# Attention's last weight steps taken apart, constants moved behind attention, and `gated @ w_out` begun in three PSUM banks without its last row block

## The chip, the cores and the metric

One core of one Trainium2 chip runs the whole program. The metric is device time in microseconds. The kernel before takes 1671.38 us (median of 3 runs, 1671.3 to 1676.62).

## The reference

Three stages follow one another on 8 batches of 576 tokens, all in float32:

```python
# attention (8 heads of 64, 128 features and their negatives)
proj = x @ w_phi;  proj = proj - max(abs(proj))
phi = concat([exp(proj), exp(-proj)])
out = (phi(q) @ (phi(k).T @ v)) / (phi(q) @ sum(phi(k)) + 1e-6)
# gated MLP
h = relu(x @ w_in);  u, v = h[..., :512], h[..., 512:]
v_n = (v - mean(v)) / sqrt(var(v) + 1e-6)
gated = u * (w_spatial @ v_n + b_spatial)
x = gated @ w_out
# mixer
u = x + (low-rank token mixing of x by U, V)
out = u + relu(u @ w_ch1) @ w_ch2
```

## The kernel before, in words

Every product of float32 operands is made of three matmuls on rounded halves: an operand is split into a high part (a copy in fp32r) and a low part (the operand less its high part), and `products` (L661) issues high x high, high x low and low x high for each row block. The functions below are named by their lines in the kernel before.

**Attention** (`attention`, L557) is a loop of 36 steps over 32 pairs of heads, in which four pairs are at different points of their way. A step projects k of the next pair (`pk`), forms the numerator and denominator of older pairs in four groups (`pn`, one bank; the copy out of it into `nd`, by DVE for group 1 and by ACT for the others, frees the bank for the next group), transposes q (`pt`) and projects q of the next pair (`pq`). DVE takes the maximum and the difference of each projection (`mk` and `sk`, `mq` and `sq`), splits the key-value product (`kv`) and copies `nd`. These are pinned: they keep the order in which the program writes them.

The weights of the next stage are brought in during these steps by a list of jobs (`weight_jobs`, L169). A job is a chain of functions; each call does one piece and returns the next. `step` calls a piece at three places of a loop step: after `less()` and `taken()` near the start, after the key features, and at the end of a step. A function marked `late` is only called at the end of a step. What is called there is put behind the newest pinned instruction of each engine (`behind`), and a new job starts at the end of a step when the last has finished. The job of the last rows of `w_spatial` and of the bias has two late pieces: `bias` (L216: ACT copies the high part, DVE subtracts, DVE clears a buffer, SP loads the bias into it) and `bias_split` (L230: ACT copies, DVE subtracts).

**Constants.** `alloc_moe` (L641) clears a buffer `w_pad`, sets two rows of it to 1 and casts it into the last rows of `vn[1]` (L653 to L656). The buffer is the weights' staging buffer. Nothing ties these instructions to a place: the scheduler that orders each engine's instructions decides.

**Gated MLP.** For each batch `gate` (L761) forms u (`pu`, four blocks f) and `w_spatial @ v_n` (`pz`, four blocks f), multiplies them and splits the product into `gs` by its four row blocks. A list of jobs runs beside it: batches 1 to 6 bring in five or six pieces of `w_ch1` and `w_ch2` each (load 512 KB, repack by ACT and DVE, store), one call of `work` behind each of the eight blocks f. Then `gated_out` (L822) makes the five token tiles of `gated @ w_out`: four of 128 tokens (`px_0` to `px_3`, 12 matmuls each, row blocks 0 to 3 in turn) and the tail (`px_4`, 8 matmuls). Each is copied by ACT to `x` and split by DVE into `xh` and `xl`, which the low-rank product `pr` reads. `pu`, `pz`, `pv`, `px` and `pt` share four PSUM banks in rotation. Between these, `values` (L711) makes v and its normal form for the next batch (`pv`, `vn`); on its path DVE and POOL (the reciprocal root `rstd`, and the low part of `vn`) alternate. In the last batch the first parts of the channel stage (`us`, `cw`) are formed on ACT and DVE at the same time.

**Channel mixing** (`channel`) follows and takes the rest of the span, from about 903 us.

## Time and profile before

| what | value |
|---|---|
| median of 3 runs | 1671.38 us |
| profiled execution | 1671.03 us, span 1669.2 us |
| PE busy | 1614.8 us, 97% of the span |
| DVE, ACT, POOL busy | 64%, 45%, 25% |
| PE's granted clock, mean | 0.988 |

The span is one profiled execution; 1.83 us of its time lie outside the span. A busy share near 100% says that the engine almost always had an instruction in hand, not that it ran at its full clock: the granted clock of a stretch (PEclk in the windows) tells that, 1.00 being 2.4 GHz and 0.50 being 1.2 GHz. What can be saved without fewer matmuls is PE's idle time and the stretches at the lower clock.

### The profile page before, as it was taken

Reading aid. Unit: us, or ns where it says so; the run is one execution under the profiler, and the core shown is the slowest. Engines: PE = TensorE matmul, PEld = TensorE weight load, DVE = VectorE, ACT = ScalarE, POOL = GpSimd, SP = SyncE. Lnnn points to the kernel's source line nnn. Section 1 sums busy time; section 2 is a strip of 40 time slices with the busy share of each in tenths; the row PEclk is TensorE's granted clock in tenths of the full one; section 3 lists DMA queues with packets and bytes.
Section 4 is the critical chain, followed back from the end, with each engine's and each line's share of the span. In section 5 each row is a group of like instructions: output and inputs, shape, how many; then the busy total and the mean of one; then the engine's idle time right before and its main releaser. Section 6 shows DMA issues by size and latency. Waiting matters only on the chain.

```text
span 1669.2 us, 28381 instructions
## 1 busy us (share of the span) xinstructions
PE 1614.8 (97%) x10968; PEld 1447.7 (87%) x10968; DVE 1072.7 (64%) x1997; ACT 744.4 (45%) x1343; POOL 421.6 (25%) x354
## 2 busy tenths in 40 slices
PE   7999998998999999999998999999999999999999
PEld 7998987887888898888897899999889999988897
DVE  6888756874567567566638885757475756565654
ACT  5888765773444443443424442323232323232322
POOL 3677774765342252342320000000000000000000
PEclk9999998999999999999999999999999999999999
DMA  4667664652132432431214441313132323232221
GB/s 136 197 198 211 202 189 125 198 148 87 59 114 86 142 109 72 123 114 62 89 46 135 130 151 52 124 54 118 60 112 65 103 72 98 71 101 76 68 85 39
DMA packets 118475, 184.53 MB, mean 111 GB/s; under 512 B 23810, under 2 KB 52642, under 8 KB 118340
## 3 DMA queue, kind: packets, MB, share of 16 engines
q1 hardware_dynamic: 118196, 182.66, 35.6%
q8 instruction: 86, 1.41, 0.4%
q14 instruction: 49, 0.40, 0.1%
q10 hardware_dynamic: 144, 0.07, 0.0%
HBM read 136.24 MB, written 36.85 MB: 104 GB/s over the span
## 4 chain that ended last, share of the span: by engine, by line
PE 72%; DMA 11%; DVE 6%; ACT 5%; issue 3%; POOL 2%; SPq 1%; DVEq 0%; POOLq 0%; ACTq 0%
PE pc L667 23%; PE ph L667 20%; DMA raw_c<-in_w_ch 5%; PE pv L667 4%; PE pn L508 4%; PE pu L667 4%; PE px L667 4%; PE pkv L480 3%; PE pk L407 2%; PE pt L439 1%; PE pt L872 1%; PE pq L407 1%; PE pz L667 1%; PE py L876 1%; DMA k<-in_kT 1%
## 5 line engine op out<-in xcount | busy, mean ns | idle before, releaser
L667 PE MATMUL pc<-h,w 128*128 128x512 f32 x1728 | 423.8, 394 | 1.5 <-ACT w L137 1.0
L667 PEld LDWEIGHTS ph<-us,cw 128*128 128x128 f32 x3024 | 384.7, 190 | 20.4 <-DVE u L993 3.1
L667 PE MATMUL ph<-us,cw 128*128 128x256 f32 x3024 | 390.0, 283 | 5.5 <-DVE u L993 4.2
L667 PEld LDWEIGHTS pc<-h,w 128*128 128x128 f32 x1728 | 314.4, 188 | 64.7 <-ACT w L137 1.2
L998 ACT ACTIVATE h<-c 128x256 fp32r<-128x256 f32 x288 | 114.6, 418 | 314.2 <-DVE c L993 307.6
L508 PE MATMUL pn<-qp,kv 128*65 128x288 f32 x768 | 211.6, 335 | 14.8 <-DVE nd L517 11.2
L461 POOL TENSOR_TENSOR qp<-e,qp 128x576 fp32r<-128x576 f32 x128 | 184.4, 1461 | 135.8 <-ACT e L458 104.3
L993 DVE TENSOR_TENSOR c<-ph,u 128x256 f32<-128x256 f32 x216 | 90.9, 422 | 111.9 <-PE ph L667 109.3
L480 PE MATMUL pkv<-v,kp 128*128 128x65 f32 x1024 | 156.9, 257 | 0.0
L480 PEld LDWEIGHTS pkv<-v,kp 128*128 128x128 f32 x1024 | 156.5, 197 | 0.0
L993 DVE TENSOR_TENSOR u<-ph,u 128x256 f32<-128x256 f32 x144 | 60.4, 422 | 146.6 <-PE ph L667 144.8
L137 ACT CAST w<-w2r 128x1024 fp32r<-128x1024 f32 x72 | 75.7, 1051 | 119.1 <-PE pc L667 106.8
L999 DVE SCALAR_TENSOR_TENSOR h<-c,h 128x256 fp32r<-128x256 f32 x288 | 115.2, 421 | 17.2 <-ACT h L998 13.4
L508 PEld LDWEIGHTS pn<-qp,kv 128*65 128x65 f32 x768 | 101.5, 143 | 21.1 <-DVE nd L517 13.0
L667 PE MATMUL pz<-wt,vn 128*128 128x288 f32 x768 | 112.3, 295 | 1.5 <-DVE u L813 1.5
L667 PE MATMUL pu<-xs,wi 128*128 128x288 f32 x768 | 105.0, 298 | 2.1 <-DVE v L730 2.1
L667 PEld LDWEIGHTS pu<-xs,wi 128*128 128x128 f32 x768 | 104.3, 190 | 3.1 <-DVE v L730 2.4
L667 PEld LDWEIGHTS pz<-wt,vn 128*128 128x128 f32 x768 | 105.3, 188 | 2.0 <-DVE u L813 2.0
L667 PE MATMUL px<-wo,g 128*128 128x512 f32 x384 | 92.4, 398 | 9.4 <-ACT g L137 9.4
L667 PEld LDWEIGHTS px<-wo,g 128*128 128x128 f32 x384 | 71.8, 191 | 27.6 <-ACT g L137 12.0
L667 PE MATMUL pv<-wi,xs 128*128 128x512 f32 x384 | 92.2, 394 | 0.0
L140 DVE TENSOR_TENSOR w<-w2r,w 128x1024 fp32r<-128x1024 f32 x72 | 88.1, 1224 | 3.1 <-ACT w L137 3.1
(150 smaller groups left out, 2255.3 us busy)
## 6 DMA issues: line engine op xcount, KB each, us to landing
w2r<-w2d SPq DMA_DIRECT2D x144, 256.0 KB, 3.0
raw_c<-in_w_ch SPq DMA_DIRECT2D x32, 512.0 KB, 4.3
v<-in_v SPq DMA_DIRECT2D x32, 325.0 KB, 4.0
k<-in_kT SPq DMA_DIRECT2D x32, 320.0 KB, 3.6
q<-in_qT SPq DMA_DIRECT2D x32, 320.0 KB, 4.1
x<-nd SPq DMA_DIRECT2D x64, 144.0 KB, 3.4
rec<-rd SPq DMA_DIRECT2D x64, 144.0 KB, 3.1
xd<-x SPq DMA_DIRECT2D x32, 288.0 KB, 2.5
```

The costliest lines, as they stand in the source:

```text
L137: nc.scalar.copy(hi, src)
L140: return (nc.gpsimd if elo == "pool" else nc.vector).tensor_tensor(out=lo, in0=src, in1=hi, op=ALU.subtract)
L407: self.pin(nc.tensor.matmul(pa[:, j * NF + t, :], x[d, t * P : (t + 1) * P], ws[d, :], start=True, stop=True,))
L439: self.pin(nc.tensor.transpose(pt[:, at, :], s[:, u, :], self.ident))
L461: self.pin(nc.gpsimd.tensor_tensor(out=lo[:, c], in0=e[:, c], in1=hi[:, c], op=ALU.subtract))
L480: self.pin(nc.tensor.matmul(pkv[:, i, j, :], kp[:, j * NF + t, :], vb[:, u * D1 : (u + 1) * D1], start=False, stop=(j == 1 and t == NF - 1),))
L508: self.pin(nc.tensor.matmul(pn, kv[k][:, i, g // 2, :], qp[q][:, i, g * HS : (g + 1) * HS], start=(m == 0), stop=(m == len(terms) - 1),))
L667: self.nc.tensor.matmul(out, x, y, start=(start and i == 0), stop=(stop and i == len(terms) - 1))
L872: nc.tensor.transpose(pt[:, s0 - c0 : s0 - c0 + n], ts[t][0][:n, fs], self.ident[:n, :n])
L993: nc.vector.tensor_tensor(out=out, in0=p, in1=q, op=ALU.add)
L998: nc.scalar.activation(hi, src, AF.Relu)
L999: nc.vector.scalar_tensor_tensor(out=lo, in0=src, scalar=0.0, in1=hi, op0=ALU.max, op1=ALU.subtract)
```

## The change

Three edits. First, in attention, the two late pieces of the bias job are cut in two, so that only ACT's copies are late; DVE's subtractions (and the clearing of the buffer with SP's load behind it) become pieces of their own that may run at the next place. Secondly, the constants of `vn` are put behind attention's last pinned instructions. Thirdly, the first three token tiles of `gated @ w_out` are opened in three banks with the row blocks 0 to 2 each, and then take row block 3 in turn; with this, the calls of `work` behind the last two blocks f move behind the low-rank product and between the two halves of `mixed`.

```diff
--- before.py
+++ after.py
@@ -119,7 +119,7 @@
         self.tail = self.S - self.NF * P
         self.NST = self.NF + 1
         self.ST = [(i * P, min(P, self.S - i * P)) for i in range(self.NST)]
-        self.pending, self.last = None, [None] * 4
+        self.pending, self.last, self.rest = None, [None] * 4, []
         dp = ctx.enter_context(tc.tile_pool(name="dp", bufs=1, space=DRAM))
         B, S = self.B, self.S
         self.xd = [dp.tile([P, self.KD, S], F32, name=f"xd{b}") for b in range(B)]
@@ -213,8 +213,15 @@
             for i in range(2):
                 nc.sync.dma_start(w[i * tail : (i + 1) * tail, :], self.w_spT[NF * P :, :])
 
+            def late(f):
+                f.late = True
+                return f
+
             def bias():
                 nc.scalar.copy(wt0, w)
+                return less
+
+            def less():
                 nc.vector.tensor_tensor(
                     out=wt1[:tail, :], in0=w[:tail, :], in1=wt0[:tail, :], op=ALU.subtract
                 )
@@ -223,14 +230,15 @@
                 for i in range(2):
                     r = tail + i * 32
                     nc.sync.dma_start(b[r : r + 1, :], self.b_sp)
-                f = lambda: bias_split(b)
-                f.late = True
-                return f
-
-            def bias_split(b):
+                return late(lambda: bias_parts(b))
+
+            def bias_parts(b):
                 for i in range(2):
                     r = slice(tail + i * 32, tail + (i + 1) * 32)
                     nc.scalar.copy(wt1[r, :], b[r, :])
+                return lambda: bias_less(b, r)
+
+            def bias_less(b, r):
                 nc.vector.tensor_tensor(
                     out=wt1[r, :], in0=b[r, :], in1=wt1[r, :], op=ALU.subtract
                 )
@@ -650,10 +658,11 @@
 
         self.vn = [mq.tile([P, self.NST, self.DH], F32R, name=f"vn{i}") for i in range(2)]
         pad = self.stage("pad", self.DH)
-        nc.vector.memset(pad[tail:, :], 0.0)
-        for r in (tail, tail + 32):
-            nc.vector.memset(pad[r : r + 1, :], 1.0)
-        nc.vector.tensor_copy(self.vn[1][tail:, NF, :], pad[tail:, :])
+        with self.behind():
+            nc.vector.memset(pad[tail:, :], 0.0)
+            for r in (tail, tail + 32):
+                nc.vector.memset(pad[r : r + 1, :], 1.0)
+            nc.vector.tensor_copy(self.vn[1][tail:, NF, :], pad[tail:, :])
 
     def gated(self, b):
         return self.mp.tile([P, 2, self.KH, self.S], F32R, tag="g", name=f"g_{b}", bufs=1)
@@ -758,22 +767,25 @@
         if f:
             f()
 
+    def work(self):
+
+
+        rest, jobs = self.rest, self.jobs
+        if rest:
+            with self.tc.issue_after(self.last[0]), self.tc.issue_after(self.last[1]):
+                f = rest.pop()()
+            if f:
+                rest.append(f)
+        if jobs and not rest:
+            rest.append(jobs.pop(0)())
+
     def gate(self, b, jobs):
-
 
         nc, mq, xs = self.nc, self.mq, self.xs
         NF, KD, HS = self.NF, self.KD, self.HS
         wi, wt, vn = self.wi, self.wt, self.vn
-        us, rest = [], []
-
-        def work():
-            if rest:
-                with self.tc.issue_after(self.last[0]), self.tc.issue_after(self.last[1]):
-                    f = rest.pop()()
-                if f:
-                    rest.append(f)
-            if jobs and not rest:
-                rest.append(jobs.pop(0)())
+        us = []
+        self.jobs = jobs
 
         for f in range(self.KH):
             u = mq.tile([P, 2, HS], F32, tag="u", name=f"u{b}_{f}", bufs=4)
@@ -793,7 +805,7 @@
             self.normalize()
             self.last[0] = act.ins
             us.append(u)
-            work()
+            self.work()
         gs = self.gs if b == 0 else self.gated(b)
         for f in range(self.KH):
             fs = slice(f * P, (f + 1) * P)
@@ -815,29 +827,38 @@
                 elo = "dve" if f == self.KH - 1 else "pool"
                 lo = self.split(gs[:, 0, f, cs], gs[:, 1, f, cs], u, elo=elo)
                 self.last[2 if elo == "pool" else 1] = lo.ins
-            work()
-        assert not jobs and not rest
+
+            if f < self.KH - 2:
+                self.work()
         self.gs, self.gt = gs, self.last_tokens(self.mp, gs, f"gt_{b}")
 
-    def gated_out(self, b, t):
-
-        nc, mp, gs = self.nc, self.mp, self.gs
-        KH, DM, NF = self.KH, self.DM, self.NF
+    def gated_open(self, b, t):
+
+        gs, KH = self.gs, self.KH
         s0, n = self.ST[t]
         px = self.psum(f"px{b}_{t}")
+        w = lambda k: [w[:, k, :] for w in self.wo]
+        pairs = [([gs[:, i, k, s0 : s0 + n] for i in range(2)], w(k)) for k in range(KH)]
+        self.products(px, pairs[:-1], stop=False)
+        return px, pairs[-1:]
+
+    def gated_out(self, b, t, begun=None):
+
+        nc, mp = self.nc, self.mp
+        DM, NF = self.DM, self.NF
+        n = self.ST[t][1]
         x = mp.tile([P, DM], F32, tag="x", name=f"x_{b}_{t}", bufs=5)
         xh = mp.tile([P, DM], F32R, tag="xh", name=f"xh{b}_{t}", bufs=3)
         xl = None
-        w = lambda k: [w[:, k, :] for w in self.wo]
         if t < NF:
+            px, last = begun or self.gated_open(b, t)
             xl = mp.tile([P, DM], F32R, tag="xl", name=f"xl{b}_{t}", bufs=3)
-            self.products(
-                px,
-                [([gs[:, i, k, s0 : s0 + n] for i in range(2)], w(k)) for k in range(KH)],
-            )
+            self.products(px, last, start=False)
             nc.scalar.copy(x, px)
             self.split(xh, xl, x, ehi="dve", elo="dve")
         else:
+            px = self.psum(f"px{b}_{t}")
+            w = lambda k: [w[:, k, :] for w in self.wo]
             low = self.tail_products(mp, px, self.gt, w, f"lowx{b}")
             nc.vector.tensor_tensor(out=x[:n], in0=px[:n], in1=low, op=ALU.add)
             self.split(xh[:n], xh[n:], x[:n], ehi="dve", elo="dve")
@@ -1143,8 +1164,11 @@
                     mx.ahead += 1
 
         mx.ahead = 0
+
+
+        begun = [mx.gated_open(b, t) for t in range(3)]
         for t in range(NST):
-            ts.append(mx.gated_out(b, t))
+            ts.append(mx.gated_out(b, t, begun[t] if t < 3 else None))
             if last and t == 0:
                 mx.combine(0)
             parts(1)
@@ -1156,8 +1180,11 @@
         mx.low_rank(pr, ts, range(3, NST))
         t1 = mx.low_rank_out(b, pr)
         ahead(1)
+        mx.work()
         mx.mixed(b, ts, t1, range(KD // 2))
         ahead(1)
+        mx.work()
+        assert not mx.jobs and not mx.rest
         mx.mixed(b, ts, t1, range(KD // 2, KD))
         ahead(1)
     for _ in pairs:
```

The first edit on DVE, in the step of `kv_21`. `sk` is the difference for k, `kv` the low part of the key-value product, `nd` the copy that frees the bank of `pn`. Before:

```order
L416 TENSOR_REDUCE mq_2986<-pq_2965 128x9
L419 TENSOR_TENSOR sq_2987<-pq_2965,mq_2986 128x1152
L218 TENSOR_TENSOR wt_100<-w_wt,wt_99 64x576
L222 MEMSET w_bs 64x576
L517 TENSOR_SCALAR nd_2990<-pn_1_3006,eps 65x288
L540 RECIPROCAL den_18_2956<-den_18_2956 128x9
L416 TENSOR_REDUCE mk_3060<-pk_3037 128x9
L419 TENSOR_TENSOR sk_3061<-pk_3037,mk_3060 128x1152
L494 TENSOR_TENSOR kv_21_3096<-pkv_2993,kv_21_3095 128x260
```

and now:

```order
L424 TENSOR_REDUCE mq_2986<-pq_2965 128x9
L427 TENSOR_TENSOR sq_2987<-pq_2965,mq_2986 128x1152
L525 TENSOR_SCALAR nd_2990<-pn_1_3006,eps 65x288
L548 RECIPROCAL den_18_2956<-den_18_2956 128x9
L424 TENSOR_REDUCE mk_3055<-pk_3032 128x9
L427 TENSOR_TENSOR sk_3056<-pk_3032,mk_3055 128x1152
L225 TENSOR_TENSOR wt_100<-w_wt,wt_99 64x576
L229 MEMSET w_bs 64x576
L502 TENSOR_TENSOR kv_21_3096<-pkv_2993,kv_21_3095 128x260
```

The subtraction and the clearing moved from ahead of `nd` to behind `sk`. The bias's own subtraction moves in the same way one step later, and the eight jobs of `w_out` come one step later each.

The second edit on DVE, where the first values are made (`st`, `mv`, `rstd`: the steps to the reciprocal root; `w_z`: zeros for the low-rank job). Before, with the two clearings far ahead, between `mk` and `sk` of attention's last full step:

```order
L656 CAST vn_4585<-w_pad 64x512
L266 MEMSET w_z 128x128
L736 BN_STATS st_0_4609<-v_0_4592 128x6
L540 RECIPROCAL den_31_4557<-den_31_4557 128x9
L737 BN_AGGR mv_0_4610<-st_0_4609 128x2
L738 TENSOR_SCALAR rstd_0_4611<-mv_0_4610 128x1
L744 TENSOR_SCALAR v_0_4592<-v_0_4592,mv_0_4610,rstd_0_4611 128x512
L139 CAST vn_4584<-v_0_4592 128x512
L736 BN_STATS st_1_4634<-v_1_4617 128x6
```

and now:

```order
L745 BN_STATS st_0_4609<-v_0_4592 128x6
L548 RECIPROCAL den_31_4557<-den_31_4557 128x9
L662 MEMSET w_pad 64x512
L746 BN_AGGR mv_0_4610<-st_0_4609 128x2
L664 MEMSET w_pad 1x512 x2
L747 TENSOR_SCALAR rstd_0_4611<-mv_0_4610 128x1
L665 CAST vn_4585<-w_pad 64x512
L753 TENSOR_SCALAR v_0_4592<-v_0_4592,mv_0_4610,rstd_0_4611 128x512
L745 BN_STATS st_1_4634<-v_1_4617 128x6
L139 CAST vn_4584<-v_0_4592 128x512
```

The three clearings now stand between the statistics of the first value tile and its root, and the cast of `vn` of tiles 0 and 1 comes behind the next tile's statistics. On POOL the low part of `vn` of tile 0 now stands behind a product of attention that waits for a load, where it stood ahead of it.

The third edit on ACT, in batch 3 behind the last part of `gs` (`gt`: the tail's columns; `low_c`: the two ACT pieces of a weight repack, the first of which waits for that weight's load). Before:

```order
L688 COPY gt_7028<-g_6862 128x4x64 x2
L838 COPY x_0_7049<-px_0_7048 128x512
L58 ACTIVATE low_c_10_6947<-raw_c_10_6909 128x512
L838 COPY x_1_7068<-px_1_7067 128x512
L76 ACTIVATE low_c_10_6947<-raw_c_10_6909 128x512
L838 COPY x_2_7087<-px_2_7086 128x512
```

and now:

```order
L697 COPY gt_7028<-g_6862 128x4x64 x2
L58 ACTIVATE low_c_10_6947<-raw_c_10_6909 128x512
L76 ACTIVATE low_c_10_6947<-raw_c_10_6909 128x512
L857 COPY x_0_7078<-px_0_7048 128x512
L857 COPY x_1_7087<-px_1_7058 128x512
L857 COPY x_2_7096<-px_2_7068 128x512
```

The copy of `px_0` moved behind both pieces of the repack, in batches 1 to 6 alike; batch 0 keeps its order on ACT. In the last batch the copies of `px_0` and `px_1` moved behind parts of `us` and `cw`.

## Rows read from the trace of the kernel before

**Rows 1.** Waits of PE over the whole span: waiter, releaser, us in total, times, longest.

```profile
PE pn L508 <- DVE nd L517: 11.2, 6, 3.9
...
PE px L667 <- ACT g L137: 9.4, 6, 1.8
```

**Rows 2.** Timeline of PE in attention: start us, us, engine line op, [idle before <-releaser].

```profile
248.05 1.16 PE L407 MATMUL pk<-wst,k 64*128 64x128 f32 x16
...
253.55 0.50 PE L508 MATMUL pn<-qp,kv 128*65 128x288 f32 x1 [3.92 <-DVE nd L517]
...
265.28 1.16 PE L407 MATMUL pk<-wst,k 64*128 64x128 f32 x16
...
270.01 0.50 PE L508 MATMUL pn<-qp,kv 128*65 128x288 f32 x1 [3.15 <-DVE nd L517]
...
282.16 1.16 PE L407 MATMUL pk<-wst,k 64*128 64x128 f32 x16
...
292.97 1.16 PE L407 MATMUL pk<-wst,k 64*128 64x128 f32 x16
```

**Rows 3.** Timeline of DVE in the same stretch.

```profile
250.23 1.95 DVE L218 TENSOR_TENSOR wt<-w_wt,wt 64x576 fp32r<-64x576 f32 x1 [2.79 <-ACT wt L217]
...
286.52 1.09 DVE L63 TENSOR_SCALAR bits_wo<-raw_wo 128x256 int32<-128x256 int32 x1
287.64 0.85 DVE L67 SCALAR_TENSOR_TENSOR bits_wo<-raw_wo,bits_wo 128x256 int32<-128x256 int32 x1
```

**Rows 4.** Two windows: us, busy us by engine, PEclk (granted clock), DMA share, GB/s.

```profile
250.00:262.00 12.00, 8.45 (x61) 8.12 (x61) 6.20 (x8) 3.33 (x6) 3.44 (x3) 0.72 0.38 108
...
359.04:375.97 16.93, 13.91 (x106) 12.57 (x105) 8.52 (x12) 9.81 (x13) 10.27 (x9) 0.80 0.26 71
```

**Rows 5.** Timeline of DVE, POOL and PE at attention's end and in the first values.

```profile
365.17 0.48 DVE L653 MEMSET w_pad<- 64x512 f32 x1 [3.15 <-POOL wo L140]
...
367.20 1.11 DVE L655 MEMSET w_pad<- 1x512 f32 x2 [0.16 <-DVE sk L419]
...
404.00 1.29 POOL L140 TENSOR_TENSOR vn<-v,vn 128x512 fp32r<-128x512 f32 x1 [1.12 <-DVE vn L139]
...
411.49 9.76 PE L667 MATMUL pu<-xs,wi 128*128 128x288 f32 x60 [2.13 <-DVE v L730]
```

**Rows 6.** Timeline of PE around px of batches 2, 3 and 6.

```profile
564.48 10.77 PE L667 MATMUL px<-wo,g 128*128 128x512 f32 x39 [1.74 <-ACT g L137]
...
623.97 2.25 PE L667 MATMUL px<-wo,g 128*128 128x512 f32 x9
627.93 9.19 PE L667 MATMUL px<-wo,g 128*128 128x512 f32 x39 [1.72 <-ACT g L137]
636.96 2.00 PE L678 MATMUL px<-wo,gt 128*128 128x512 f32 x8
...
808.67 2.25 PE L667 MATMUL px<-wo,g 128*128 128x512 f32 x9
```

**Rows 7.** Timeline of ACT around px of batches 1, 3 and 6.

```profile
513.19 0.69 ACT L58 ACTIVATE low_c<-raw_c 128x512 int32<-128x512 uint32 x1 [3.49 <-DMA raw_c<-in_w_ch]
...
515.15 0.66 ACT L76 ACTIVATE low_c<-raw_c 128x512 f32<-128x512 f32 x1 [0.81 <-DVE bits_c L71]
...
631.17 0.58 ACT L838 COPY x<-px 128x512 f32<-128x512 f32 x1
...
632.80 0.68 ACT L58 ACTIVATE low_c<-raw_c 128x512 int32<-128x512 uint32 x1 [1.05 <-DMA raw_c<-in_w_ch]
...
818.82 0.69 ACT L58 ACTIVATE low_c<-raw_c 128x512 int32<-128x512 uint32 x1 [2.00 <-DMA raw_c<-in_w_ch]
```

**Rows 8.** Timeline of DVE and ACT around px of the last batch.

```profile
874.70 0.69 DVE L140 TENSOR_TENSOR xl<-x,xh 128x512 fp32r<-128x512 f32 x1
...
876.95 0.43 DVE L139 CAST xh<-x 128x512 fp32r<-128x512 f32 x1 [1.56 <-ACT x L838]
...
878.00 1.14 ACT L137 CAST us<-u 128x512 fp32r<-128x512 f32 x2 [1.08 <-DMA u<-ud]
```

## Prediction

> **What bounds the kernel now.** I read PE's waits first, since PE is busy 97% of the span: only its idle time and its slow stretches are to be had. Two lines of that view lie where the change works: the second numerator bank waited 11.2 us for DVE's `nd`, 3.9 us at worst, and `px` waited 9.4 us in six places for ACT's part of `gs` [rows 1]. Then the timeline of PE shows what a long wait costs beyond itself. A full step of attention runs from one `pk` to the next; the last one listed takes 292.97 - 282.16 = 10.81 us, while the two ahead of it take 265.28 - 248.05 = 17.23 and 282.16 - 265.28 = 16.88 [rows 2]. The waits of 3.92 and 3.15 us in them explain a little over half of the 6.42 and 6.07 us excess. The rest is the clock: the window around the first wait had a granted clock of 0.72, the one at attention's end 0.80 [rows 4], where 1.00 is 2.4 GHz and 0.50 is 1.2 GHz. In both, PE had just stood idle for 2 to 4 us. So a wait in attention is paid about twice.
>
> Why PE waited is in DVE's timeline: the subtraction of the tail weights ran from 250.23, behind ACT's copy, for 1.95 us [rows 3], with the clearing and `nd` queued behind it, and PE's next `pn` needs the bank that `nd` frees.
>
> **The change part by part.**
>
> *Bias steps.* The subtractions leave the place ahead of `nd` and go behind `sk`, ahead of `kv`. Nothing is added to any engine. In the new place DVE does 1.95 us and the clearing, and for the bias at most as much again (half the partitions). Is that place free? The step from 282.16 to 292.97 answers it: there DVE did 1.09 + 0.85 us of weight work and one more piece in this very place [rows 3], and it is the 10.81 us step [rows 2]. So I book both excesses as saved, 6.42 + 6.07 = 12.5, less 0.3 for a slightly late `kv`: **-12.2 us**. The bounds: if the late `kv` made PE wait as `nd` did, nothing is saved (0); more than 12.5 can't be, as these are all that the two steps lose. SP's load of the bias comes nearer to ACT's copy that reads it; if it lands late, ACT waits with some 2 us in hand before its next `nd` (an estimate from the steps' order). The later jobs of `w_out` shift by one step and cost what they cost.
>
> *Constants.* Before, the first clearing stood between `mk` and `sk` and waited 3.15 us for POOL's last reader of the staging buffer [rows 5]; everything of that step waited with it. From that step's `pk` to the next numerator group passed 16.93 us at a clock of 0.80 [rows 4]. A full step is 10.81, and I leave 0.6 for the hand-over of the bank at its end: 16.93 - 10.81 - 0.6 = 5.5. The last piece of `w_out` now runs in that step, for which I take off 0.3: **-5.2 us**. Bounds: 0 if something else stops that step, 5.5 at most.
>
> What is late next are the values. The clearings, 0.48 + 1.11 = 1.59 us [rows 5], now stand ahead of the first `rstd`, on the chain that alternates between DVE and POOL. POOL then takes attention's product first, which waits for its load, and the low part of `vn`, 1.29 us [rows 5], comes behind it. At the end of this chain DVE frees the bank for which PE already waits 2.13 us at 411.49 [rows 5]. Bounds: 0, if the load hides the shift; 1.59 + 1.29 = 2.9, if both go through. As the order puts `vn` behind a load that ends when it ended before, its 1.29 goes through whole, and one statistics pass more lies ahead of a cast: I take **+2.0 us**, nearer to the upper end.
>
> *`px`.* In batch 3 PE did 9 matmuls from 623.97, waited 1.72 for row block 3, and did 39 from 627.93 to the tail at 636.96, 9.03 / 39 = 0.23 us each [rows 6]: full pace, so this wait did not lower the clock. Only in batch 2 did the 39 take 10.77 instead of 9.19, so 1.6 more [rows 6]. Now 27 matmuls (6.2 us) lie ahead of row block 3, longer than the wait's end (627.93 - 623.97 = 3.96 after the start): the wait goes. Without another one, 48 + 8 + 6 matmuls for `px` and the first part of `pr` would take 62 x 0.23 = 14.3 us, against 636.96 + 14 x 0.23 - 623.97 = 16.2 before, 1.9 less per batch.
>
> But the copy of `px_0` now stands behind the repack. In batch 3 the weight landed at 632.80 [rows 7]; the second ACT piece ends 515.15 + 0.66 - 513.19 = 2.62 after a landing [rows 7], so at 635.4; the copy takes 0.58 [rows 7] and frees the bank at 636.0. `px_4` needs that bank, and would want it at 623.97 + 48 x 0.23 = 635.0: a new wait of 1.0. DVE follows: the repack's last piece (0.69), three `xh` of 0.43 and three `xl` of 0.69 [rows 8] from 635.4 end at 639.5, and the last `pr` can start no sooner, ending at 639.7 against 640.2 before: 0.5 saved, not 1.9. I take 0.6 for batches 1, 3, 4 and 5, whose weights land alike, and 0.6 + 1.6 = 2.2 for batch 2. In batch 6 the weight landed at 818.82, 10.15 after `px` began at 808.67 [rows 6, 7], 1.3 later than in batch 3: about 0.6 lost. Sum: -2.4 - 2.2 + 0.6 = **-4.0 us**. Bounds: -13, if the copies don't wait (6 x 1.9 + 1.6); +11, if each of six new waits costs 2.5 beyond itself in clock, as 3.92 us did in attention (6.42 - 3.92 = 2.5; -4.0 + 6 x 2.5).
>
> Here the Trainium skill speaks against the change: "TensorE: Matmul & The Clock Gate", section "A second HAM failure mode: psum-queue depth-cycling", says that short idles between groups of matmuls that cycle through the PSUM banks can make the clock swing between its levels and cost throughput. By that rule the six new bank waits would be paid twice, which is the third rival below; the rows of batch 3 don't bear it out, those of batch 2 do.
>
> *Calls of `work`.* Only batches 1 and 2 have a sixth piece that reaches the moved calls; the ACT order there stays behind `x_2`, so 0.
>
> *Last batch.* `xh_0`, `xl_0` and `xh_1` (0.43 + 0.69 + 0.43 = 1.55) were done by 877.4, while DVE waited; now they come behind parts that need the load which landed at 878.00 [rows 8]. From there DVE is busy until PE's next waits end, so **+1.4 us**, between 0 and 1.55.
>
> **Sum.** -12.2 - 5.2 + 2.0 - 4.0 + 1.4 = -18.0, on the profiled execution's 1671.03: 1653.0. The median of the runs is 0.35 above that execution, so 1653.4 us.
>
> **Rivals.**
> 1. *The wait on `px` goes and nothing takes its place*: the copies of `px` don't hold PE, the weight landing sooner. For it: PE's order has 18 matmuls (4.1 us) between `px_0`'s end and `px_4`. Against it: 8.8 us from start to landing in batch 3 [rows 6, 7]. 1653.4 - 9 = 1644.
> 2. *Attention's stall moves instead of going*: the subtraction delays `kv`, POOL's work beside it stretching it further, and PE waits at the key-value products. For it: 1.95 us for 64 x 576 [rows 3] is long. Against it: the 10.81 us step. 12.2 come back: about 1665.6, less than 0.4% under the time before.
> 3. *Slower*: in six batches PE waits at `px_4` for the bank and the clock falls to 1.2 GHz behind the wait. At 0.50 every 0.23 us matmul costs 0.23 more. The saving elsewhere, 18.0, is used up when each batch loses 3.0 us more than I booked, that is when some 13 matmuls a batch run at 1.2 GHz; a whole block of 24 value matmuls more at that clock gives 6 x 5.5 = 33 and 1686. Against it: waits of 1.72 left the clock alone in batch 3 [rows 6]. For it: batch 2, and the new wait of batch 6 would be over 2 us.
> 4. *The order rows don't show on the chip*, as the edit to attention leaves the jobs one step later and something unseen is late: 1671.
>
> **How the numbers follow.** My forecast, with its bounds mixed, 0.68; rival 1, 0.11; rival 2, 0.11; rival 3, 0.06, half of it above the old time; rival 4, 0.04. The range of 1645 to 1663 takes in the forecast with its unknown terms (values 0 to 2.9, `px` from -9 to +6 around its value) and most of rival 1. A measurement of this kernel can tell about 0.3% from no change, 5.0 us: faster means under 1666.4. Forecast, rival 1 and most of rival 2 are: 0.90. Within 0.3%: the rest of rival 2, rival 4 and a little of rival 3, 0.07. Slower: 0.03.
>
> **What would show it.** In the profile after: no wait of PE on `nd` over 1.6 us (one of 1.56 at another weight's job is untouched); steps of 10.8 to 11.3 us where 17.23 and 16.88 stood; no 2.4 us hole in the last full step; PE's wait on DVE's `v` grown from 2.13 to about 4; `px` no longer waiting for `g`, but `px_4` or `pr` waiting for ACT's `x` and DVE's `xl`, 1 to 2.5 us in each of batches 1 to 6; 1.4 us later at the channel stage's first products. It would be wrong if PE waits on `kv` by 2 us or more in the two steps, or if the windows of `px` show a granted clock under 0.9 in most batches.

## The result, and the profile after

The changed kernel takes 1652.02 us (median of 3 runs, 1650.5 to 1657.8): 0.9878 of the time before, 95% interval 0.9852 to 0.9904. Forecast were 1653.4 us and a range of 1645 to 1663. A second measurement beside another kernel (experiment 5) gave 1653.40 us, 0.9897 [0.9868, 0.9925]. So it is faster by about 19 us, well over the 5.0 us that can be told from no change.

The profiled execution took 1650.5 us, span 1648.7, against 1671.03 and 1669.2: 20.5 less. PE's waits, as waiter, releaser, us in total, times, longest:

```profile
PE pn L516 <- DVE nd L525: 5.4, 5, 1.5
PE px L687 <- ACT x L857: 4.9, 6, 1.1
...
PE pu L676 <- DVE v L739: 3.3, 1, 3.3
```

Beside [rows 1]: the waits of 3.9 and 3.15 on `nd` are gone and the longest left is 1.5; the six waits of `px` for `g`, 9.4 us, are gone too, and six new ones stand there, 4.9 us in all, of the tail `px_4` for ACT's copy `x`. The wait for `v` grew from 2.13 [rows 5] to 3.3.

The two bias steps, in PE's timeline (the places of [rows 2]) and DVE's (the place of [rows 3]):

```profile
248.10 1.16 PE L415 MATMUL pk<-wst,k 64*128 64x128 f32 x16
...
258.75 1.16 PE L415 MATMUL pk<-wst,k 64*128 64x128 f32 x16
...
269.38 1.16 PE L415 MATMUL pk<-wst,k 64*128 64x128 f32 x16
```

```profile
251.18 1.36 DVE L427 TENSOR_TENSOR sk<-pk,mk 128x1152 f32<-128x1152 f32 x1
252.46 1.18 DVE L225 TENSOR_TENSOR wt<-w_wt,wt 64x576 fp32r<-64x576 f32 x1
253.88 0.54 DVE L229 MEMSET w_bs<- 64x576 f32 x1 [0.24 <-PE pn L516]
254.67 0.43 DVE L502 TENSOR_TENSOR kv<-pkv,kv 128x260 fp32r<-128x260 f32 x1 [0.25 <-ACT kv L501]
```

The steps take 10.65 and 10.63 where 17.23 and 16.88 stood. The subtraction is behind `sk` now, and with 1.18 us instead of 1.95 it ends before `kv`'s other input is there (DVE waits 0.25 for ACT). Two windows, with the columns of [rows 4]:

```profile
250.00:262.00 12.00, 12.00 (x121) 11.22 (x120) 9.48 (x11) 9.64 (x13) 8.27 (x7) 1.00 0.58 165
345.85:374.09 28.24, 24.75 (x194) 22.27 (x193) 11.76 (x18) 18.51 (x28) 20.70 (x16) 0.88 0.36 107
```

The clock in the first is 1.00, where 0.72 was granted. The second window is the last step with all that follows it up to the first value product: 28.24 us. Before, that step began at 359.04 [rows 4] and the first value product stood here, 391.57 - 359.04 = 32.53 later:

```profile
391.57 11.16 PE L667 MATMUL pv<-wi,xs 128*128 128x512 f32 x48
```

`px` of batch 3, on PE and on ACT:

```profile
603.61 11.16 PE L676 MATMUL px<-wo,g 128*128 128x512 f32 x48
615.60 2.12 PE L687 MATMUL px<-wo,gt 128*128 128x512 f32 x8 [0.83 <-ACT x L857]
617.55 0.39 PE L871 MATMUL pr<-xh,ua 128*128 128x512 f32 x1
...
619.13 5.66 PE L676 MATMUL pv<-wi,xs 128*128 128x512 f32 x24
```

```profile
612.39 0.68 ACT L58 ACTIVATE low_c<-raw_c 128x512 int32<-128x512 uint32 x1 [1.58 <-DMA raw_c<-in_w_ch]
614.41 0.66 ACT L76 ACTIVATE low_c<-raw_c 128x512 f32<-128x512 f32 x1 [1.34 <-DVE bits_c L71]
614.98 2.03 ACT L857 COPY x<-px 128x512 f32<-128x512 f32 x4
```

All 48 products run without a hole, where one of 1.72 stood before [rows 6]. On ACT the copies stand behind the second half of a repack, and when it ends at 614.98 all four run in one piece: they had been ready. The first of them frees the bank on which `px_4` waited 0.83.

Set side by side at the same places of both timelines, the distance to the kernel before grows and shrinks like this: -17.5 at the first value product, -16.4 at the first `pz`, -17.55 at the first `px` of batch 0 and still -17.55 at that of batch 1, -22.4 at the first `px` of the last batch, -20.5 at the end.

### The profile page after: what moved, and what is told of

Its sections match the earlier page's. It is cut to its first block, busy times and chain, and to the rows that moved or that the text cites. A ratio compares the mean times of both kernels' runs of the same rounds, so it can differ in the third digit from the quotient of the medians.

```text
span 1648.7 us, 28379 instructions
## 1 busy us (share of the span) xinstructions
PE 1605.4 (97%) x10968; PEld 1436.9 (87%) x10968; DVE 1073.5 (65%) x1997; ACT 744.0 (45%) x1343; POOL 421.4 (26%) x354
## 4 chain that ended last, share of the span: by engine, by line
PE 72%; DMA 11%; DVE 6%; ACT 5%; issue 2%; POOL 2%; SPq 1%; DVEq 0%; ACTq 0%; POOLq 0%
PE pc L676 23%; PE ph L676 21%; DMA raw_c<-in_w_ch 6%; PE pn L516 4%; PE pu L676 4%; PE pv L676 4%; PE pkv L488 4%; PE pz L676 2%; PE pk L415 2%; PE pt L447 1%; PE pt L893 1%; PE pq L415 1%; ACT low_c L76 1%; DMA w_wt<-in_w_spT 1%; DVE bits_c L71 1%
## 5 line engine op out<-in xcount | busy, mean ns | idle before, releaser
L516 PE MATMUL pn<-qp,kv 128*65 128x288 f32 x768 | 208.3, 332 | 9.0 <-DVE nd L525 5.4
L488 PE MATMUL pkv<-v,kp 128*128 128x65 f32 x1024 | 152.5, 252 | 0.0
L488 PEld LDWEIGHTS pkv<-v,kp 128*128 128x128 f32 x1024 | 151.1, 191 | 0.0
L676 PE MATMUL px<-wo,g 128*128 128x512 f32 x384 | 88.8, 390 | 0.0
L438 ACT ACTIVATE kp<-sk 128x1152 f32<-128x1152 f32 x64 | 74.5, 1165 | 27.8 <-DVE sk L427 19.9
```

The source lines that it names most:

```text
L438: self.pin(self.nc.scalar.activation(kp, self.st[p]["sk"], AF.Exp, scale=1.0 - 2.0 * i))
L488: self.pin(nc.tensor.matmul(pkv[:, i, j, :], kp[:, j * NF + t, :], vb[:, u * D1 : (u + 1) * D1], start=False, stop=(j == 1 and t == NF - 1),))
L516: self.pin(nc.tensor.matmul(pn, kv[k][:, i, g // 2, :], qp[q][:, i, g * HS : (g + 1) * HS], start=(m == 0), stop=(m == len(terms) - 1),))
L676: self.nc.tensor.matmul(out, x, y, start=(start and i == 0), stop=(stop and i == len(terms) - 1))
```

## The experiments

Single stages of an execution vary by one to three us from run to run (which batch loses clock, how late a load lands), and the kernel before ranged from 1659 to 1685 us on the chips of these runs. So the stages are read from the traces, and the medians only tell kernels apart that differ by more.

| kernel | median us (runs) | ratio to before, 95% |
|---|---|---|
| bias steps alone | 1654.82 (6) | 0.9886 [0.9860, 0.9911] |
| constants alone | 1667.77 (12) | 0.9961 [0.9946, 0.9976] |
| `px` alone | 1669.02 (12) | 0.9960 [0.9942, 0.9977] |
| changed, repack behind | 1646.50 (5) | 0.9835 [0.9813, 0.9858] |
| changed, last batch as before | 1653.20 (5) | 0.9867 [0.9848, 0.9887] |
| changed, constants behind the values | 1657.01 (5) | 0.9890 [0.9869, 0.9912] |
| changed without constants' edit | 1649.15 (5) | 0.9850 [0.9821, 0.9879] |
| the same again | 1649.58 (6) | 0.9875 [0.9847, 0.9902] |
| changed again | 1653.40 (6) | 0.9897 [0.9868, 0.9925] |
| combined | 1640.69 (5) | 0.9816 [0.9789, 0.9842] |
| combined, casts behind `nd` | 1641.02 (5) | 0.9818 [0.9788, 0.9848] |
| combined, calls later | 1641.90 (6) | 0.9832 [0.9803, 0.9861] |

### 1. The three edits one by one

Each is the kernel before with one part of the diff.

Bias steps alone (the core of the edit: the subtraction becomes a call of its own):

```diff
             def bias():
                 nc.scalar.copy(wt0, w)
+                return less
+
+            def less():
                 nc.vector.tensor_tensor(
```

> The kernel before with the bias steps' edit alone: the two subtractions behind the step's difference, not ahead of nd. Theory (the wait and the clock behind it both go): the steps of 17.23 and 16.88 become 10.6 to 10.8, PE has no wait on nd above 1.6, the time falls by 12 to 13.5, to about 1658.5. Rival (the stall moves to the key-value products): PE waits on kv by 2 or more in those steps and the time falls by less than 5. Rival (only the stalls of 3.92 and 3.15 go and the clock was low for another reason): the steps end at 13 to 14 and the time falls by about 7.

The profiled span fell by 16.4 (1669.2 to 1652.8), more than the theory's 13.5; by the medians of its chip the time fell by 19 (15 to 23). So by the medians this edit alone (0.9886) can't be told from the whole change (0.9878 and 0.9897). No step of 17 us is left and `nd` is waited for 1.4 at the longest, so both rivals fall. But the extra is the surprise of this case: the hole of [rows 5] is gone as well, with the constants' code untouched. DVE and POOL at the end of attention:

```profile
356.00 1.36 DVE L427 TENSOR_TENSOR sq<-pq,mq 128x1152 f32<-128x1152 f32 x1
...
364.22 0.48 DVE L661 MEMSET w_pad<- 64x512 f32 x1 [5.38 <-POOL wo L140]
364.87 1.11 DVE L663 MEMSET w_pad<- 1x512 f32 x2 [0.16 <-PE pn L516]
366.02 0.43 DVE L502 TENSOR_TENSOR kv<-pkv,kv 128x260 fp32r<-128x260 f32 x1
```

```profile
363.33 0.72 POOL L140 TENSOR_TENSOR wo<-w_wo,wo 128x256 fp32r<-128x256 f32 x1
```

The clearing still waits for POOL's last reader of the staging buffer, now 5.38 us instead of 3.15. Yet `mk`, `sk`, `mq` and `sq` of the last step are done by then: the bias job takes one step more, all jobs of `w_out` move one step back, and the clearing, which follows the last job, lands behind that step's `sk` and `sq` instead of ahead of them. Of that step's work on the projections only `kv` stands behind it. From the last step's `pk` at 347.31 to the first value product at 374.29 passed 26.98, against 32.53 before.

Constants alone:

```diff
-        nc.vector.memset(pad[tail:, :], 0.0)
+        with self.behind():
+            nc.vector.memset(pad[tail:, :], 0.0)
```

> The kernel before with the constants' edit alone: clearing and ones of the pad behind attention. Theory: from the last step's pk to the first value product 32.5 shrinks to 28.2, as in the changed kernel; then PE waits for v some 3.3 instead of 2.13, and the wait of 1.14 for u at the end of the gate goes in exchange, so nothing of it is given back: the time falls by 4 to 4.5, to about 1667. Rival (the prediction's own: the value chain gets 2.0 longer and that stays): the time falls by 2 to 3.

The profiled span fell by 3.4. From the last step's `pk` to the first value product passed 26.87 (358.91 to 385.78), 5.7 less, so the first half of the theory holds. But 4.10 were waited for `v`, and from the first value product to `px` of batch 0 passed 47.39 instead of 45.77: what the clearing costs among the statistics stays, as the rival, the prediction's own account, had it. The size stays open: 3.4 lies between the two, and the medians of this chip say 6.5 (4.0 to 9.0), more than either.

`px` alone (the core of the edit):

```diff
+        begun = [mx.gated_open(b, t) for t in range(3)]
         for t in range(NST):
-            ts.append(mx.gated_out(b, t))
+            ts.append(mx.gated_out(b, t, begun[t] if t < 3 else None))
```

> The kernel before with the px edit alone (three row blocks opened, the last weight block in the last place, two calls of work later). Theory: per batch 0 to 2.3 saved, 4.9 over batches 1 to 6, with a new wait of px_4 for ACT's copy x of 0.4 to 1.1 in each; the last batch loses 1.9: the time falls by 3, to about 1668.4. Rival (the wait only changes its name): PE's idle time in px stays at 9.4 and the time is unchanged or higher, above all if the clock falls behind px_4's wait (below 0.95 in the windows of px).

The span fell by 3.2, but 1.7 of it was there at the first value product (389.85 against 391.57), in attention, which this edit leaves as it was, and 2.4 at the first `px` of batch 0 (434.89 against 437.34). The waits of `px` for `g` are replaced by those of its tail for ACT:

```profile
PE px L678 <- ACT x L848: 5.5, 6, 1.1
```

From the first `px` of batch 1 to that of the last batch 3.5 were gained, and 2.7 lost from there to the end: 0.8 net in this profile, where the theory had 3. The medians of this chip say 6.7 (3.9 to 9.7), so one profile of each does not settle the size. Part of the gain is clock, which the two kernels without this edit show. In them, as before, PE waits in the midst of `px`; here the first row is of the bias kernel, batch 4, the other two of the constants kernel, batches 2 and 4:

```profile
670.56 10.79 PE L675 MATMUL px<-wo,g 128*128 128x512 f32 x39 [1.73 <-ACT g L137]
```

```profile
560.15 10.71 PE L668 MATMUL px<-wo,g 128*128 128x512 f32 x39 [1.95 <-ACT g L137]
...
685.27 10.80 PE L668 MATMUL px<-wo,g 128*128 128x512 f32 x39 [1.73 <-ACT g L137]
```

39 products take 9.2 at full pace [rows 6]. In the three profiles with this wait, 4 of 18 such blocks took about 1.6 longer, in batch 2 or 4 and twice in each; over each of these four blocks the granted clock was 0.84. So the 1.6 of batch 2 in [rows 6] doesn't come in every execution: the bias kernel's batch 2 took 9.20 after a wait of 1.88.

By the medians the three edits alone save 19.1 + 6.5 + 6.7 = 32 us, and the whole change 20. The hole that two of them remove accounts for some 5.5 of the difference; the rest is about what the intervals allow.

### 2. Who holds px_4

In the changed kernel the repack call after the gate moves behind the five output tiles; on ACT and DVE the copies and splits of `px` come ahead of it:

```diff
-            if f < self.KH - 2:
+            if f < self.KH - 3:
                 self.work()
...
+            self.last[0] = nc.scalar.copy(x, px).ins
+            self.last[1] = self.split(xh, xl, x, ehi="dve", elo="dve").ins
...
             parts(1)
+        mx.work()
         pr = mx.psum(f"pr{b}", "b")
```

> The changed kernel with the repack call that follows the gate put behind the five output tiles, so that the copies of px come ahead of it on ACT. Theory (px_4 waits for its bank because px_0's copy stands behind a repack): the six waits of 0.4 to 1.1, 4.9 in all, go, from px's start to the next batch's values passes 14.2 to 14.6 instead of 15.5, and the time falls by 4 to 7 against the changed kernel. Rival (DVE's halves xh and xl are as late as the copies): the wait only moves to pr, and the time falls by 0 to 2. Rival (the weights come too late and the next batch's jobs stand in the gate's way): the time rises.

1646.50 us, 0.9835 [0.9813, 0.9858]; the profiled execution is 4.5 under that of the changed kernel. `px` of batch 3, on PE and on ACT:

```profile
603.48 11.12 PE L676 MATMUL px<-wo,g 128*128 128x512 f32 x48
614.44 2.00 PE L687 MATMUL px<-wo,gt 128*128 128x512 f32 x8
...
617.64 5.67 PE L676 MATMUL pv<-wi,xs 128*128 128x512 f32 x24
```

```profile
611.02 1.55 ACT L857 COPY x<-px 128x512 f32<-128x512 f32 x3
614.64 0.59 ACT L857 COPY x<-px 128x512 f32<-128x512 f32 x1 [2.06 <-PE px L676]
615.12 0.66 ACT L58 ACTIVATE low_c<-raw_c 128x512 int32<-128x512 uint32 x1
```

None of the six bank waits is left, and the values start 617.64 - 603.48 = 14.16 after `px`, against 619.13 - 603.61 = 15.52. Over batches 1 to 6 that is 7.7 us. About half is given back: in batches 1 and 2 a sixth weight is repacked later and the tail of the values waits for ACT's copy of `uo`,

```profile
PE pv L687 <- ACT uo L900: 2.4, 2, 1.2
```

and three times the next gate waits 0.6 to 0.8 for `u`. So the place behind the repack held PE, as the prediction said, and PE's wait names ACT's copy. The edit moves DVE's halves with the copies, so it doesn't show whether they would have been the next limit in their old place.

### 3. The last batch

```diff
-        begun = [mx.gated_open(b, t) for t in range(3)]
+        begun = [] if last else [mx.gated_open(b, t) for t in range(3)]
```

> The changed kernel with the three opened row blocks in all batches but the last, which keeps the order of before. Theory (opened blocks put the last batch's first halves behind parts that wait for a load): what the last batch loses goes, 1.5 to 2 less than the changed kernel. Rival (that load sets the end of the batch either way): within 0.5 of it.

From `px` of the last batch to the eight transposes that wait for ACT's copy of `uo` the kernel before takes 901.91 - 870.65 = 31.26. PE's timeline of the kernel before, of the changed kernel, then of this one:

```profile
870.65 11.08 PE L667 MATMUL px<-wo,g 128*128 128x512 f32 x48
...
901.91 1.43 PE L872 MATMUL pt<-ident,x 128*128 128x128 f32 x8 [0.32 <-ACT uo L879]
```

```profile
848.25 11.08 PE L676 MATMUL px<-wo,g 128*128 128x512 f32 x48
...
881.10 1.43 PE L893 MATMUL pt<-ident,x 128*128 128x128 f32 x8 [0.32 <-ACT uo L900]
```

```profile
850.59 11.08 PE L676 MATMUL px<-wo,g 128*128 128x512 f32 x48
...
881.95 1.43 PE L893 MATMUL pt<-ident,x 128*128 128x128 f32 x8 [0.32 <-ACT uo L900]
```

32.85 in the changed kernel, 31.36 here: 1.5 come back, and by the end of the program 1.9 (800.45 and 798.51 from `px` of the last batch). The total doesn't show it, mainly because this run's first batch took 3.0 longer than the changed kernel's first profile: 48.7 from the first value product to `px`, with 4.64 waited for `v`. That led to experiments 4 and 5.

### 4. The constants, elsewhere or undone

Behind the last statistics, in the gate's first products:

```diff
-        with self.behind():
-            nc.vector.memset(pad[tail:, :], 0.0)
...
+        def constants():
+            with self.tc.issue_after(self.last[1]):
+                nc.vector.memset(pad[tail:, :], 0.0)
...
             self.normalize()
+            if b == 0 and f == 0:
+                self.constants()
```

> The changed kernel with the constants of the pad not among the first value statistics but behind the last of them, in the gate's first products. Theory (the clearing lengthens the chain of statistics by what stands in it, 1.6 and a cast): PE's wait for v falls from 3.3 to about 2, and the time by 1.2. Rival (DVE then comes to u as late as in the kernel before, where PE waited 1.14 at the gate's end): the wait for u comes back and the time stays within 0.3.

The rival holds, and by more than it said. The wait for `v` fell to 1.87, but at the gate's end PE waited 1.82 for `u`, where DVE now had the clearing besides the repacks of `U` and `V`. From the first value product to `px` passed 48.2, no less than with the clearing among the statistics (45.7 to 48.7, experiment 5).

Undone, that is, the change without this edit:

> The changed kernel without the constants' edit. Theory (the bias edit alone moved the weights' jobs one step later and with them the clearing, as its run by itself shows): no hole comes back in the last step, PE waits 2.0 for v instead of 3.3, and the time is 0 to 1.5 lower than the changed kernel's. Rival (the prediction: the constants' edit is worth 5.2 less 2.0 by itself): the hole of 2.4 and its clock are back and the time is 3 to 5 higher.

1649.15 us. No hole in the last step (28.15 from its `pk` to the first value product), 1.64 waited for `v`, 44.9 from there to `px`. The profiled execution, 1654.04, stands above the median: a load for one of `w_spatial`'s casts landed late, the cast stood ahead of `nd`, and the step took 15.7. DVE and PE there:

```profile
228.21 1.09 DVE L139 CAST wt<-w_wt 128x576 fp32r<-128x576 f32 x1 [3.86 <-DMA w_wt<-in_w_spT]
229.22 0.50 DVE L525 TENSOR_SCALAR nd<-pn,eps 65x288 f32<-65x288 f32 x1
```

```profile
229.78 0.35 PE L516 MATMUL pn<-qp,kv 128*65 128x288 f32 x1 [3.26 <-DVE nd L525]
```

This is the same queue as in the bias steps, one weight earlier; the change does not touch it. The second profile of this kernel has such a step too (15.65), where the changed kernel's two have 12.3 and 12.4; what makes the load late was not found.

### 5. The two again, on one chip

> The changed kernel once more, beside the one without the constants' edit on the same chip. Theory (the clearing among the statistics costs 2 to 3, and the first profile of the changed kernel hid it): PE's wait for v is 3.3 to 4.6, and from the first value product to px of the first batch pass 47 to 49, where the first profile had 45.7. Rival (the first profile is typical and the constants cost nothing there): 45.5 to 46.

> The changed kernel without the constants' edit, once more. Theory: wait for v 1.6 to 2.6, 44.5 to 45.5 from the first value product to px, no hole in the last step; 1 to 3 lower than the changed kernel on the same chip. Rival: within 0.5 of it, or higher, as the hole of the kernel before comes back in some runs.

1653.40 and 1649.58 us: 3.8 apart, though their intervals overlap. PE's wait for `v` and the 60 products behind it, of the changed kernel the first time, of it again, and of the one without the constants' edit:

```profile
395.15 9.74 PE L676 MATMUL pu<-xs,wi 128*128 128x288 f32 x60 [3.26 <-DVE v L739]
```

```profile
394.75 10.83 PE L676 MATMUL pu<-xs,wi 128*128 128x288 f32 x60 [3.95 <-DVE v L739]
```

```profile
395.18 8.21 PE L675 MATMUL pu<-xs,wi 128*128 128x288 f32 x60 [0.64 <-DVE v L738]
```

The stretch to `px` took 45.7, 47.3 and 43.8. In all profiles but the one with the clearing in the gate, before included, the five with the clearing among the statistics took 45.7, 47.3, 47.4, 47.7 and 48.7 (mean 47.4) for it; the eight with the clearing in attention took 43.8 to 45.8 (mean 44.9). So the clearing among the statistics costs 2.5 there, and with the bias edit in place the constants' edit saves next to nothing in attention (28.24 and 26.98 in the two profiles of the changed kernel, 28.15 in both without). The first profile of the changed kernel was the most favourable of the five.

### 6. Taken together

The changed kernel with the constants' edit undone, the repack behind the tiles, and the last batch as before:

> The changed kernel with three things taken together: the constants' edit undone, the repack call behind the five output tiles, and no opened blocks in the last batch. Theory (the three act in different stages): no clearing among the value statistics, wait for v 1.6 to 2.5 instead of 3.3 to 4.6, about 2 less from the first values to px; 4.5 less by the repack; 2.4 less in the last batch: 6 to 9 under the changed kernel, about 1643. Rival (in the first batch the wait for u takes back what the wait for v gave, and the last batch waits for its load anyway): as the repack alone, 1646.

1640.69 us, 0.9816 [0.9789, 0.9842]: below the kernel before and the changed one, 11 us under the latter, and the theory's sum (6 to 9) is a little exceeded. 44.6 us pass from the first value product to `px`, and no wait of `px` is left. PE's longest waits behind attention are now

```profile
PE ph L675 <- DVE u L1013: 4.2, 2, 2.8
...
PE pv L686 <- ACT uo L899: 2.4, 2, 1.3
...
PE pu L675 <- DVE v L738: 2.2, 1, 2.2
```

Two further edits to it:

```diff
-            work = step(work, True)
             taken()
+            work = step(work, True)
```

> The combined kernel, and in attention the weights' last call of a step behind the taking of the numerator, so that on DVE a cast that waits for its load no longer stands ahead of nd. Theory (what is left of PE's waits on nd, 1.4 to 3.3 in three steps, is that cast): waits on DVE's nd of over 1 go and the steps of 12.2 become 10.7 to 10.9: 4 to 5 less than the combined kernel. Rival (mk of the next step then waits instead, and with it kv): the steps keep their 12 and PE waits on kv; 0 to 2 more.

1641.02 us, no difference. The waits on `nd` fell from 4.0 to 1.2, but the steps with a cast still take 11.5 to 12.2, now with the waits on `kv` at 4.5 instead of 2.3: the rival. DVE stands at the same late load either way, and a place in the queue only chooses who waits.

```diff
-        mx.work()
         mx.mixed(b, ts, t1, range(KD // 2))
+        mx.work()
         ahead(1)
-        mx.work()
-        assert not mx.jobs and not mx.rest
         mx.mixed(b, ts, t1, range(KD // 2, KD))
+        mx.work()
```

> The combined kernel with the last two repack calls each half a mixing later. Theory (in the first two long batches the sixth weight's load and repack hold back the store and copy of uo, and the tail of the values waits 1.2 for that): those two waits go, 2 to 3 less than the combined kernel. Rival (the store queue is as full half a mixing later, or the next gate's jobs then come late): within 1 of it, the waits moved to the next gate.

1641.90 us, no difference either: the two waits for `uo` shrank from 1.3 and 1.2 to 0.8 and 0.6, and 1.1 for `u` came in the first gate, as the rival had it. The combined kernel is the best one measured.

## Why the prediction was right, point by point

**Bias steps (-12.2).** Right. The two steps lost 34.11 - 21.28 = 12.8, stall and clock, and the place behind `sk` was free. Rival 2, a stall that moves to `kv`, fell.

**Constants (-5.2).** The size was about right, the cause wrong. From the last step's `pk` to the first value product 4.3 are gone in the first profile and 5.55 in the second; with the two steps and 0.4 from others that makes the 17.5 that are gone up to the first value product, where -12.2 - 5.2 = -17.4 were booked. But the hole was booked to the constants' edit, and the bias edit removes it alone (26.98 against 32.53), by moving the clearing one step's worth down DVE's queue. The step that failed is "The last piece of `w_out` now runs in that step, for which I take off 0.3": it saw the shift of the jobs, and not that the clearing shifts with them. The sum could not show this error, since both edits were made; only the runs of parts did. For the change without this edit the same working would have said 1653.4 + 5.2 - 2.0 = 1656.6, and 1649.15 and 1649.58 were measured.

**Values (+2.0).** Right in kind, and nearly in size: the wait for `v` rose to 3.3 in the first profile and 3.95 in the second, where about 4 was said. The stretch was 0.1 shorter than before in the first profile, since DVE was not late for `u` at the gate's end (1.14 before) and the clock behind the wait fell no deeper, and 1.5 longer in the second. The mean loss of the profiles with the clearing here, against those with it in attention, is 2.5.

**`px` (-4.0).** From the first `px` of batch 1 to that of the last batch -4.85 in the first profile and -1.9 in the second. Over the seven profiles with the edit and its bank waits it is -3.4 in the mean against the profile of before, and -4.6 against the mean of the three profiles with the old wait. Booking 1.6 for batch 2 counted on a low clock that some executions have there and others have not; that the first profile comes so near is in part luck. The new wait at `px_4` was there in each of the six batches, 0.4 to 1.1 in the first profile where 1.0 was worked out, for the reason given; the sign that the prediction gave, 1 to 2.5, was too high. From `px` to the values, batches 1 to 6 of the first profile gained 1.1, 2.3, 0.7, 0.2, 0.0 and 1.0, where 0.6, 2.2, 0.6, 0.6, 0.6 and -0.6 were booked; 0.4 of the sum was given back between the batches. Mis-sized is batch 6: its weight landed 795.88 - 787.34 = 8.5 us after `px` began, not the 10.15 that was taken over from the trace of before [rows 6, 7].

**Last batch (+1.4).** 1.6 to those eight transposes (2.0 in the second profile) and 1.9 to the end; undoing it gives 1.9 back. The term was sized a little short.

**Sum.** -18.0 against -20.5 in the first profile and -16.4 in the second (1654.59). The median lies between them, 1.4 under the forecast the first time and on it the second. The sum is no evidence for each of its terms: the bias edit gives what was booked to the constants besides its own, and the constants' edit, booked at -5.2 + 2.0, costs some 2.5 beside it.

**Rivals.** Rival 1 (nothing takes the place of `px`'s wait) fell; experiment 2 shows its price, 7.7 before give-backs and 4.5 in the profile, where it was given 9. Rival 3 (the bank waits cost clock) fell: in the seven profiles with them there are 42 waits of 0.3 to 1.4, and the window over each of these 42 batches' `px`, `pr` and first values had a granted clock of 1.00. The rule of the Trainium skill's "TensorE: Matmul & The Clock Gate", section "A second HAM failure mode: psum-queue depth-cycling", by which such idles make the clock swing, is not borne out by these waits. The prediction read batch 2 of [rows 6] as bearing it out, but the 18 waits of 1.25 to 1.95 in the midst of `px` are for an operand within a group, not for a bank between groups. Four of them cost clock, and none tests the rule. Rival 4 fell.

## What to carry to other kernels

A job taken apart into more calls shifts everything that is queued behind it in the same list; before a second edit is credited with removing a wait, look where the first alone puts the waiting instruction. On an in-order engine an instruction that waits for a load or a slow engine should stand behind those that free PSUM banks, as the subtraction behind `nd` and the repack behind the copies of `px` did; moving it only to another place of the same wait (the casts, the constants) hands the wait to the next reader. Run parts of a change alone: here one of three edits, a gain by itself, turned out to cost some 2.5 us in its stage beside another, and without it, with two small repairs, the kernel came to 1640.69 us.

## What the runs showed of the hardware

The same subtraction of 64x576 took 1.95 us in [rows 3] and 1.18 in the changed kernel, and the traces show what goes with it: the product that POOL was at when it started. POOL before, and in the changed kernel; then DVE in the combined kernel with the casts behind `nd`, where POOL was idle:

```profile
250.16 1.41 POOL L461 TENSOR_TENSOR qp<-e,qp 128x576 fp32r<-128x576 f32 x1
```

```profile
251.61 1.42 POOL L469 TENSOR_TENSOR qp<-e,qp 128x576 fp32r<-128x576 f32 x1
```

```profile
251.34 0.74 DVE L225 TENSOR_TENSOR wt<-w_wt,wt 64x576 fp32r<-64x576 f32 x1
```

POOL's product ended at 251.57 before and at 253.03 after, and the subtraction ended 0.61 behind it both times. So it is in all eleven profiles in which a product of POOL was running when the subtraction started (0.61 or 0.62); in the three others it took 0.74. In its old place it met the product at its start in all three profiles (1.94 to 1.97), behind `sk` in its second half or not at all (0.74 to 1.22). So what rival 2 said of POOL's work fits these rows, but the new place met less of it. No run changes POOL's work alone.

How deep the clock falls behind a wait of PE varies with the wait in these rows. The 60 products behind the wait for `v` took 8.21 at a granted clock of 1.00 after waits of 0.64 and 1.64; 9.6 to 9.8 at 0.82 to 0.84 after waits of 1.87 to 3.26 (eight profiles); and 10.3 to 10.8 at 0.73 to 0.78 after 3.95 to 4.64 (four). So the longer waits cost 1.4 to 2.6 more in the products that followed. In `px`, waits of about the same 1.7 us sometimes cost 1.6 more and mostly nothing, and what decides between them stays open.
